# Tile loads in halves, released 48 records behind the begins of TensorE's 256-record blocks

## Chip, cores and metric

One core of a Trainium2 chip runs the whole kernel. The metric is the device time of one execution in microseconds. Before and after are compared by the medians of several runs.

## What is computed

Retention over q, k and v (8 batches, 8 heads, 576 positions, 64 per head, fp32), and then a mixture of experts with two levels of routing: 4 groups of 4 experts, one expert per token, 4608 tokens of 512 values, a hidden layer of 1024.

```python
# retention
scores = q @ k.transpose(0, 1, 3, 2) / sqrt(64)
gamma  = 1 - 2.0 ** (-5 - arange(8))
rel    = pos[:, None] - pos[None, :]
x      = (scores * where(rel >= 0, gamma ** rel, 0)) @ v
# mixture of experts, for each token of x (4608 x 512)
g = argmax(x @ w_group);  e = argmax(x @ w_expert[g])
y = softmax weight of g * softmax weight of e * (relu(x @ w1[g, e]) @ w2[g, e])
```

## The kernel before

**Two stages.** The first computes the retention of 36 tiles of 128 tokens (NT = 36, nine to a pair of batches; the ninth, marked m, holds the last 64 tokens of both) and routes their tokens. The second runs the experts' two layers, one pass per expert. The change lies in the first.

**One step per tile.** The loop at L968 goes over t from 0 to 36. Step t issues to TensorE, in this order: `av(t - 1)` (L911, the products of scores and values, eight matmuls into px), `state(t)` (L890, the product of keys and values, pst), `inter(t - 1)` (L926, what the state adds to px), `scores(t + 1)` (L842, into pss), the transposition of tile t - 6 (`xnat_pe`, L430, pxt), and every third step the logits and the routing of a group of three tiles. In the first steps the order differs a little. Tiles marked m have no state of their own. `scale(t + 1)` (L833) lets ScalarE multiply that tile's values before. VectorE masks the scores and turns px into x. GpSimd stores the rows of x into `xs`, sorted by expert, with indirect DMAs.

**Order.** All engines but TensorE are wrapped in `Ordered` (L113): what they are given keeps the order of the program, SP's loads too. TensorE is scheduled by hand, in program order (`pe = nc.tensor`, L129). Since every operation of a wrapped engine is recorded in the wrapper, rows of ScalarE, VectorE, GpSimd and SP have L124.

**Loads.** A tile is 1 MB in fp32: two planes of q and k, transposed, and two of v and k (`a`, tag "r", 7 buffers, RB). `loads(t)` (L727) issues it on SP, most tiles in one DMA of 1 MB; tiles 0, 1, 2 and the m tiles come in two DMAs. Before the loop six tiles are asked for (LOADS - 1, L809). In step t, behind `av(t - 1)`, `loads(t + 6)` (L989) follows. Its buffer was that of tile t - 1, so SP waits there until the last reader of that tile is done; where no `inter` reads it, a dependency on its `av` is added by hand.

**First weights.** The expert with the most tokens so far is chosen in step 28 (`pick`, PICK = 23, r = t - 23 = 5), and its number is read into a register of SP in step 29 (`expert_of(0)`, L1034). `xload(0)` in step 30 asks for its rows, and waits for their stores. `load_piece(0)` to `load_piece(3)` in steps 30 to 33 (L1042) ask for four weight pieces of 1 MB, in the same ring of buffers as the tiles, behind `xload(0)` on SP. `layer1(0, 0)` (L1047) uses the first piece in step 35.

**Matmuls as records.** The profile has one weight load and one matmul for a transposition or for a matmul of bf16 or fp32r operands, and two of each for a matmul of fp32: the eight of `av` stand as x16.

Of the kernel before, what the change touches and what calls it, by code (L numbers as in the profile page):

```python
# [7 lines left out]
F32 = mybir.dt.float32  # L8
# [7 lines left out]
P = 128  # L16
RG = 3
B, H, S, D = 8, 8, 576, 64
# [16 lines left out]
PICK = 23  # L35
WHOLE = 2
RB = 7
LOADS = 7
WARM = 7
TURNED = 2  # L40

FULL = 5
# [30 lines left out]
def moe_retention(ctx, tc, qkv, wgt, w, c_f, out):  # L73
# [52 lines left out]

            return call

    pe = nc.tensor  # L129
    dve, act, pool, sp = [Ordered(e_) for e_ in (nc.vector, nc.scalar, nc.gpsimd, nc.sync)]  # L130

    def apart(key, inst):
# [586 lines left out]
    with ExitStack() as ac:  # L719
# [4 lines left out]
        pss = ps_s.tile([P, 2, 4 * P], F32, name="pss")  # L724
        ps_x = ac.enter_context(tc.tile_pool(name="ps_x", bufs=1, space=PSUM))

        def loads(t):  # L727
            if t >= NT:
                return
            T = tiles[t]  # L730
            a = wp.tile([P, 4, DM], F32, name=f"a_{t}", tag="r", bufs=RB)
            n = 3 if T["m"] else 4
            if t < 2:
                flat = qkv[t].rearrange("h p c d -> (h p c d)")
                for i, j in (0, 2), (2, 3):
                    part = flat[i * P * DM : j * P * DM]
                    sp.dma_start(a[:, i:j], part.rearrange("(p c d) -> p c d", p=P, c=j - i))
            else:
                if t == 2:
                    for i in range(2):  # L740
                        i_ = sp.dma_start(a[:, 2 * i : 2 * i + 2], qkv[t, i])
                elif T["m"]:
                    sp.dma_start(a[:, 2:3], qkv[t, 1, :, 0:1])
                    i_ = sp.dma_start(a[:, 0:2], qkv[t, 0])
                else:
                    i_ = sp.dma_start(
                        a.rearrange("p (h c) d -> p h c d", h=2), qkv[t].rearrange("h p c d -> p h c d")
                    )
            u = t - RB
            if u > 0 and tiles[u]["S"] == [None]:  # L750

                tc.add_manual_dep(
                    i_.ins, tiles[u]["av"].name,
                    mybir.DependencyInfo(mybir.DependencyClass.Sync, mybir.DependencyReason.DATA),
                    reason="one tile a step",
                )
            T["qT"], T["kT"] = [a[:, i].rearrange("p (i j) -> p i j", i=NP) for i in range(2)]
            T["v"], T["k"] = [a[:, i].rearrange("p (h d) -> p h d", h=H) for i in (2, 3)]

        masks = dc.tile([P, 2, 2, P], F32, name="masks")  # L760
        rel = masks[:, 1].bitcast(I32)
# [44 lines left out]
        make_masks()  # L806
        act.dma_start(cf[:, 0:KC_ID], c_f[:, 0:KC_ID])
        act.activation(warm, warm, AF.Exp)
        for t in range(LOADS - 1):  # L809
            loads(t)  # L810

            if t == 3:
                sp.dma_start(wgp, wgt.rearrange("p (c e) -> p c e", c=NKC))
                sp.dma_start(cf[:, KC_EID:KC_TRI], c_f[:, KC_EID:KC_TRI])
# [27 lines left out]
        def scores(t):  # L842

            T = tiles[t]
            T["pss"] = pss
            if t == 0:
                T["pss"] = ps_x.tile([P, 2, 4 * P], F32, name="pss_0", tag="x")
            ps = T["pss"]  # L850
            whole = NP if t < FULL else 0
            for i in range(0, NP - whole, 2):
                for late in range(2):
                    for par in range(2):
                        for o in range(2):
                            k_ = slice((late ^ par) * D, (late ^ par) * D + D)
                            r = slice(o * D, o * D + D)
                            to = late * D + D if T["m"] else P
                            pe.matmul(  # L859
                                ps[k_, o, (i + par) * P + late * D : (i + par) * P + to],  # L860
                                T["kT"][r, i + par, k_], T["qT"][r, i + par, late * D : to],
                                start=True, stop=True,
                            )
            for i in range(NP - whole, NP):
                for o in range(2):
                    r = slice(o * D, o * D + D)
                    pe.matmul(  # L867
                        ps[:, o, i * P : i * P + P], T["kT"][r, i, :], T["qT"][r, i, :],
                        start=True, stop=True,
                    )  # L870
# [11 lines left out]
        def kturn(t):  # L882

            T = tiles[t]
            pk = ps_tr.tile([P, NP, P], F32, name=f"pk_{t}", tag="tr")
            for i in range(NP):
                pe.transpose(pk[:, i, :], T["kT"][:, i, :], ident)
            act.copy(T["k"].rearrange("p (i o) d -> p i (o d)", o=2), pk)

        def state(t):  # L890

            T = tiles[t]
            if T["m"]:
                T["S"] = [cur.pop(0)[1], cur.pop(1)[1]]
                return
            bi = T["j"] // 4
            first = bi not in cur
            T["S"] = [None if first else cur[bi][1]]
            pst = ps_st.tile([P, NP, D], F32, name=f"pst_{t}", tag="tr") if first else cur[bi][0]
            for i in range(NP):  # L900
                for o in range(2):
                    h = 2 * i + o
                    pe.matmul(  # L903
                        pst[o * D : o * D + D, i, :], T["k"][:, h, :], T["vs"][:, h, :],
                        start=first and i == 0, stop=True, skip_group_check=True,
                    )
            st = ap.tile([P, NP, D], F32, name=f"st_{t}", tag="st", bufs=5)
            act.copy(st, pst)
            cur[bi] = (pst, st)

        def av(t):  # L911

            T = tiles[t]
            px = ps_x.tile([P, 2, 4 * P], F32, name=f"px_{t}", tag="x")
            for s in range(2):
                for o in range(2):
                    for g in range(2):
                        T["av"] = pe.matmul(  # L918
                            px[g * D : g * D + D, o, s * P : s * P + P],
                            T["vs"][:, 4 * s + 2 * g + o, :], T["sT"][:, o, 2 * s + g, :],  # L920
                            start=s == 0, stop=True, skip_group_check=True,
                        )
            T["av"] = T["av"].ins
            T["px"] = px

        def inter(t):  # L926
# [38 lines left out]
        masked(0)  # L965
        first_gq((6,))
        kturn(0)
        for t in range(NT + 1):  # L968
            now = t < NT
            r = t - PICK  # L970

            if last_of_group(t - 4):
                choose(t - 4)
# [12 lines left out]
                scale(t + 1)  # L986
            if t:
                av(t - 1)
            loads(t + LOADS - 1)  # L989
            if 0 < t < TURNED:  # L990
                kturn(t)
            if now and not opening:
# [45 lines left out]
            if r == 11:  # L1038
                pick(1)
                expert_of(1)  # L1040
            if 6 < r < 11:
                load_piece(r - 7)  # L1042
            if t == NT - 1:
                load_piece(4, tiles[t - 6]["row"])
            if t == NT - 1:

                layer1(0, 0)  # L1047

    mc = ExitStack()
    psy = mc.enter_context(tc.tile_pool(name="psy", bufs=1, space=PSUM))  # L1050
    mp = mc.enter_context(tc.tile_pool(name="mp", bufs=2))
# [596 lines left out]
```

## Time and profile before

| | us |
|---|---|
| median of 3 runs | 563.97 |
| lowest, highest | 563.22, 566.93 |
| the profiled execution, its own time | 565.27 |
| its span, first to last instruction | 563.40 |
| TensorE matmuls busy in it | 548.6 (97%) |
| VectorE, ScalarE, GpSimd busy | 426.0, 330.4, 258.3 |

The span is what the profile's rows cover; the profiled execution's own time is 1.87 us more. The granted clock of TensorE was 0.998 of full speed over the span. TensorE's busy time counts matmuls from their start to a modelled end, so they overlap; an idle time of its row is time in which no matmul was under way. PE is TensorE's matmuls, PEld its weight loads.

### The profile page before, as it was taken

What the parts mean: (1) busy time and instruction counts of PE and PEld (TensorE: products, weight loads), DVE (VectorE), ACT (ScalarE), POOL (GpSimd) and SP (SyncE); (2) the same over time, 40 slices, a digit from 0 to 9 for tenths busy, and PEclk for the clock granted to TensorE, in tenths of its full rate; (3) what the DMA queues carried; (4) which work ended last, traced back from release to release, by engine and by line L of the source; (5) the groups of instructions that cost most, each with busy time, mean ns of one, the idle gap of its engine ahead of it and who ended that gap; (6) DMA issues with size and microseconds to landing.
All of it is one profiled execution on the core that took longest, in us unless ns stands there. A gap on an engine that the chain in (4) does not pass through costs nothing.

```text
span 563.4 us, 16624 instructions
## 1 busy us (share of the span) xinstructions
PE 548.6 (97%) x6149; PEld 520.8 (92%) x6149; DVE 426.0 (76%) x1000; ACT 330.4 (59%) x858; POOL 258.3 (46%) x394
## 2 busy tenths in 40 slices
PE   8998999899999999999999999999999999999995
PEld 6887888788689999999999999999999999999995
DVE  6886777788889678976767686877778687787783
ACT  7687877787565545454545454555555455555563
POOL 0023323253521138454554638373664836638565
PEclk9999999999999999999999999999999999999999
DMA  8998999969766893837465674839476584855831
GB/s 337 416 409 313 311 375 325 356 227 333 263 205 262 222 330 84 322 107 292 131 275 149 259 234 174 301 119 340 108 297 205 200 283 141 337 186 216 298 144 43
DMA packets 51001, 139.84 MB, mean 248 GB/s; under 512 B 7922, under 2 KB 28154, under 8 KB 42193
## 3 DMA queue, kind: packets, MB, share of 16 engines
q1 hardware_dynamic: 41648, 118.28, 58.9%
q0 software_dynamic: 9104, 20.07, 9.8%
q8 instruction: 73, 1.20, 0.8%
q14 instruction: 32, 0.25, 0.1%
q10 hardware_dynamic: 144, 0.05, 0.0%
HBM read 118.31 MB, written 24.55 MB: 254 GB/s over the span
## 4 chain that ended last, share of the span: by engine, by line
PE 95%; issue 2%; POOL 1%; DMA 1%; SPq 0%; POOLq 0%; ACT 0%; ACTq 0%
PE ph L695 35%; PE py L1147 11%; PE py L1146 11%; PE py L1148 11%; PE px L918 7%; PE pss L859 4%; PE pxt L437 4%; PE px L937 3%; PE pst L903 3%; PE py L1135 2%; PE plt L487 2%; PE phn L1203 1%; POOL out L124 1%; DMA a<-in_qkv 1%; PE pss L867 1%
## 5 line engine op out<-in xcount | busy, mean ns | idle before, releaser
L124 POOL DMA_INDIRECT out<-y,ii x148 | 161.1, 1089 | 58.8 <-issue 29.2
L124 DVE TENSOR_TENSOR wl<-r,wh 128x512 fp32r<-128x512 f32 x268 | 172.5, 685 | 6.0 <-ACT wh L124 3.1
L124 ACT ACTIVATE hh<-ph 128x320 fp32r<-128x320 f32 (+14 forms) x128 | 53.4, 417 | 182.1 <-PE ph L695 134.9
L124 ACT CAST wh<-r 128x512 fp32r<-128x512 f32 x268 | 151.7, 617 | 1.1 <-DMA r<-in_w 1.1
L695 PE MATMUL ph<-xTh_m,wh 128*128 128x316 f32 (+14 forms) x504 | 147.3, 292 | 0.0
L695 PE MATMUL ph<-xTl_m,wh 128*128 128x316 f32 (+13 forms) x504 | 147.3, 292 | 0.0
L695 PE MATMUL ph<-xTh_m,wl 128*128 128x316 f32 (+13 forms) x504 | 146.7, 291 | 0.0
L1147 PE MATMUL py<-hh,wl 128*128 128x316 f32 (+11 forms) x480 | 140.4, 293 | 0.0
L1146 PE MATMUL py<-hh,wh 128*128 128x316 f32 (+14 forms) x480 | 140.3, 292 | 0.0
L1148 PE MATMUL py<-hl,wh 128*128 128x316 f32 (+11 forms) x480 | 139.9, 291 | 0.0
L124 DVE SCALAR_TENSOR_TENSOR hl<-ph,hh 128x320 fp32r<-128x320 f32 (+13 forms) x126 | 58.0, 460 | 84.3 <-ACT hh L124 83.8
L695 PEld LDWEIGHTS ph<-xTh_m,wh 128*128 128x128 f32 x504 | 94.9, 188 | 0.7 <-issue 0.3
L695 PEld LDWEIGHTS ph<-xTl_m,wh 128*128 128x128 f32 x504 | 95.0, 188 | 0.2
L695 PEld LDWEIGHTS ph<-xTh_m,wl 128*128 128x128 f32 x504 | 95.0, 188 | 0.0
L1147 PEld LDWEIGHTS py<-hh,wl 128*128 128x128 f32 x480 | 90.4, 188 | 0.0
L1148 PEld LDWEIGHTS py<-hl,wh 128*128 128x128 f32 x480 | 90.3, 188 | 0.0
L1146 PEld LDWEIGHTS py<-hh,wh 128*128 128x128 f32 x480 | 90.3, 188 | 0.0
L124 POOL COPY pace<-hh 1x1 f32<-1x1 f32 x137 | 32.3, 236 | 119.7 <-ACT hh L124 119.0
L124 POOL DMA_INDIRECT xs<-xt,sl x33 | 32.6, 989 | 92.6 <-DVE xT L124 35.0
L124 ACT ACTIVATE vs<-a,cf 128x64 f32<-128x64 f32 x288 | 72.4, 336 | 2.7 <-DMA a<-in_qkv 2.7
L124 DVE TENSOR_TENSOR sT<-pss,masks 128x512 f32<-128x512 f32 x72 | 46.1, 682 | 9.4 <-PE pss L859 6.6
L918 PE MATMUL px<-sT,vs 128*64 128x128 f32 x576 | 39.5, 279 | 0.4 <-issue 0.3
(210 smaller groups left out, 611.3 us busy)
## 6 DMA issues: line engine op xcount, KB each, us to landing
r<-in_w SPq DMA_DIRECT2D x68, 1024.0 KB, 8.8
a<-in_qkv SPq DMA_DIRECT2D x29, 1024.0 KB, 9.5
xb<-xs SPq DMA_DIRECT2D x32, 165.0 KB, 3.9
a<-in_qkv SPq DMA_DIRECT2D x8, 512.0 KB, 6.5
xb<-xs SPq DMA_DIRECT2D x20, 148.5 KB, 3.3
out<-y,ii POOLq DMA_INDIRECT x148, 2.8
a<-in_qkv SPq DMA_DIRECT2D x6, 256.0 KB, 5.2
xb<-xs SPq DMA_DIRECT2D x8, 132.0 KB, 3.0
```

What stands on the lines that cost most here:

```text
L124: i_ = f(*a, **k)
L437: pe.transpose(T["pxt"][:, i, :], T["xT"][:, i, :], ident)
L487: pe.matmul(plt[32 * i : 32 * i + 32], wgp[:, i, :], tiles[t]["xTg"][:, i], start=True, stop=True)
L695: pe.matmul(ph[:, :v], a[:, kc, cs], b[:, kc, :v], start=n == 0, stop=n == 3 * NKC - 1)
L859: pe.matmul(ps[k_, o, (i + par) * P + late * D : (i + par) * P + to], T["kT"][r, i + par, k_], T["qT"][r, i + par, late * D : to], start=T ...
L903: pe.matmul(pst[o * D : o * D + D, i, :], T["k"][:, h, :], T["vs"][:, h, :], start=first and i == 0, stop=True, skip_group_check=True,)
L918: T["av"] = pe.matmul(px[g * D : g * D + D, o, s * P : s * P + P], T["vs"][:, 4 * s + 2 * g + o, :], T["sT"][:, o, 2 * s + g, :], start=s ...
L937: pe.matmul(px[g * D : g * D + D, o, s * P + r * w : s * P + r * w + w], st[rows, 2 * s + g, :], T["qT"][rows, 2 * s + g, r * w : r * w + ...
L1135: pe.matmul(py[:n], a[:, r0 : r0 + n], b[:, f % 2, :], start=st_ and m == 0, stop=sp_ and m == len(ab) - 1,)
L1146: pe.matmul(py[:, :w0], wh[:, f % 2, ds_], hh[:, :w0], start=st_, stop=False)
L1147: pe.matmul(py[:, :w], wl[:, f % 2, ds_], hh[:, :w], start=False, stop=False)
L1148: pe.matmul(py[:, :w], wh[:, f % 2, ds_], hl[:, :w], start=False, stop=sp_)
```

## The change

`Blocks` wraps TensorE and counts records: 2 for each call, 4 for a matmul whose stationary operand is plain fp32, 1 more by hand in `scores` and in `state`. Whenever the count passes 240 + 256 k, the instruction that passed it is given to `block`. `block` works out how far the loads may be asked: the step, plus the share of the step that is done (175 records to a step), plus a lead of 5.0 that grows to 5.8 over the first 25 steps, and not further than five tiles ahead of the step's own. Up to there it issues half tiles (`load(t, part)`, part 0 q and k, part 1 v and k), and weight pieces behind the tiles; each of these DMAs waits on SP until that instruction of TensorE is done. The call of `loads` in the step, the dependency on `av` and the pieces of steps 30 to 33 are gone. The six tiles ahead of the loop remain, as halves. What is still unasked of the four pieces is asked in step 35.

```diff
-LOADS = 7
 WARM = 7
+BLOCK, BLOCK0 = 256, 192 + 48
+FIRST = 6
+LEAD = (5.0, 0.8, 25)
...
-    pe = nc.tensor
+    class Blocks:
+
+        def __init__(self, engine, begin):
+            self.engine, self.n, self.turn = engine, begin, None
+
+        def records(self, n):
+
+            new = (self.n + n - BLOCK0) // BLOCK > (self.n - BLOCK0) // BLOCK
+            self.n += n
+            return new
+
+        def __getattr__(self, name):
+            f = getattr(self.engine, name)
+
+            def call(*a, **k):
+                i_ = f(*a, **k)
+                wide_ = name == "matmul" and a[1].dtype == F32
+                if self.records(4 if wide_ else 2) and self.turn:
+                    self.turn(i_)
+                return i_
+
+            return call
+
+    pe = Blocks(nc.tensor, 2)
...
-        def loads(t):
-            if t >= NT:
-                return
+        def load(t, part, behind=None):
+
             T = tiles[t]
-            a = wp.tile([P, 4, DM], F32, name=f"a_{t}", tag="r", bufs=RB)
...
+            if part == 0:
+                a = T["a"] = wp.tile([P, 4, DM], F32, name=f"a_{t}", tag="r", bufs=RB)
...
+            if t < TURNED:
                 flat = qkv[t].rearrange("h p c d -> (h p c d)")
...
+                i, j = ((0, 2), (2, 3))[part]
+                i_ = sp.dma_start(
+                    a[:, i:j], flat[i * P * DM : j * P * DM].rearrange("(p c d) -> p c d", p=P, c=j - i)
+                )
+            elif T["m"] and part:
+                i_ = sp.dma_start(a[:, 2:3], qkv[t, 1, :, 0:1])
             else:
...
-                    i_ = sp.dma_start(
-                        a.rearrange("p (h c) d -> p h c d", h=2), qkv[t].rearrange("h p c d -> p h c d")
-                    )
-            u = t - RB
-            if u > 0 and tiles[u]["S"] == [None]:
+                i_ = sp.dma_start(a[:, 2 * part : 2 * part + 2], qkv[t, part])
+            if behind is not None:
 
                 tc.add_manual_dep(
-                    i_.ins, tiles[u]["av"].name,
+                    i_.ins, behind.name,
                     mybir.DependencyInfo(mybir.DependencyClass.Sync, mybir.DependencyReason.DATA),
...
+        asked = {"half": 2 * FIRST, "piece": 0}
+
+        def block(i_):
+
+            t = now_at["t"]
+            far = t + (pe.n - now_at["n"]) / 175 + LEAD[0] + LEAD[1] * min(1, t / LEAD[2])
+            while asked["half"] < min(int(2 * far), 2 * (t + 6), 2 * NT):
+                load(*divmod(asked["half"], 2), i_.ins)
+                asked["half"] += 1
+            while asked["piece"] < min(int(far + 0.5) - NT, NPIECE):
+                load_piece(asked["piece"], i_.ins)
+                asked["piece"] += 1
+
+        now_at = {}
...
-        for t in range(LOADS - 1):
-            loads(t)
+        for t in range(FIRST):
+            for part in range(2):
+                load(t, part)
...
             T = tiles[t]
+            pe.records(1)
             T["pss"] = pss
...
             first = bi not in cur
+            if t >= TURNED:
+                pe.records(1)
...
         kturn(0)
+        pe.turn = block
         for t in range(NT + 1):
             now = t < NT
             r = t - PICK
+            now_at.update(t=t, n=pe.n)
...
                 av(t - 1)
-            loads(t + LOADS - 1)
...
-            if 6 < r < 11:
-                load_piece(r - 7)
             if t == NT - 1:
+                while asked["piece"] < NPIECE:
+                    load_piece(asked["piece"])
+                    asked["piece"] += 1
                 load_piece(4, tiles[t - 6]["row"])
...
+    pe.turn = None
```

## Rows read from the trace of the kernel before

**Rows 1.** Busy time by stretch (us, busy us of each engine with instructions, PEclk, DMA share, GB/s)

```profile
0.00:20.00 20.00, 18.21 (x291) 14.02 (x295) 13.38 (x32) 14.51 (x53) 1.13 (x9) 1.00 0.92 361
...
120.00:140.00 20.00, 19.70 (x465) 16.74 (x460) 17.35 (x56) 15.77 (x55) 8.39 (x16) 1.00 0.79 272
...
160.00:540.00 380.00, 380.00 (x2907) 378.22 (x2906) 289.31 (x608) 198.92 (x428) 198.61 (x289) 1.00 0.65 227
```

**Rows 2.** Waits of TensorE's matmuls, 10 to 140 us (total us, times, longest)

```profile
PE pss L859 <- issue: 5.0, 5, 2.0
PE pxt L437 <- issue: 0.9, 1, 0.9
PE px L918 <- issue: 0.3, 1, 0.3
PE pst L903 <- issue: 0.3, 1, 0.3
```

**Rows 3.** Busy time by stretch, cut at the ends of TensorE's gaps (engines as in rows 1: PE, PEld, DVE, ACT, POOL)

```profile
22.51:28.24 5.73, 4.85 (x134) 4.28 (x131) 5.03 (x16) 3.23 (x15) 0.00 (x0) 1.00 1.03 415
28.24:39.48 11.24, 10.54 (x255) 8.84 (x254) 9.04 (x28) 9.51 (x34) 3.47 (x5) 1.00 1.02 407
...
46.16:52.54 6.38, 5.09 (x127) 4.47 (x127) 5.03 (x16) 4.10 (x16) 1.60 (x5) 1.00 0.92 307
52.54:74.69 22.15, 21.58 (x509) 18.51 (x509) 16.61 (x44) 17.49 (x61) 6.79 (x11) 1.00 0.91 320
103.56:110.57 7.01, 5.00 (x132) 4.29 (x128) 5.03 (x16) 5.05 (x20) 2.15 (x3) 1.00 0.99 366
110.57:126.73 16.16, 16.14 (x379) 14.10 (x383) 13.03 (x40) 12.23 (x43) 7.72 (x18) 1.00 0.70 253
```

**Rows 4.** Chain that ended last, 0 to 140 us (start, us, what; each px begins a step)

```profile
24.35 1.02 PE px L918 x16
...
27.36 0.89 issue
...
32.78 1.02 PE px L918 x16
...
44.43 1.02 PE px L918 x16
...
51.26 1.29 issue
...
68.49 1.02 PE px L918 x16
...
74.13 0.57 issue
...
79.77 1.02 PE px L918 x16
...
108.56 2.03 issue
...
115.99 1.02 PE px L918 x16
...
138.27 1.09 PE px L918 x16
```

**Rows 5.** DMA queues, 25.9 to 27.0 us (packets, MB, share of 16 engines)

```profile
q8 instruction: 1, 0.02, 5.4%
```

**Rows 6.** DMA queues: first line 20 to 36 us, the others 36 to 120 us

```profile
DMA packets 1769, 6.55 MB, mean 410 GB/s; under 512 B 113, under 2 KB 113, under 8 KB 1765
...
q1 hardware_dynamic: 5841, 21.83, 74.3%
q0 software_dynamic: 1831, 6.19, 18.7%
```

**Rows 7.** SP's instructions in order of time, 112 to 150 us (start, us, merged)

```profile
125.77 2.69 SPq L124 DMA_DIRECT2D xb<-xs  x4
...
129.79 17.62 SPq L124 DMA_DIRECT2D r<-in_w  x5
```

## Prediction of the time after

> **What bounds the kernel now.** I looked first at the table of stretches. From 160 to 540 us TensorE is busy 380.00 of 380.00 us, at a granted clock of 1.00, so nothing can be won there except by an earlier start. From 0 to 140 us it is not: 18.21 us in the first 20 and 19.70 in the last [rows 1]. The change lies in that first stage, where each of the 36 steps does the retention of one tile.
>
> Next I asked what TensorE waits for between 10 and 140 us. Four lines answer: 5.0, 0.9, 0.3 and 0.3 us, 6.5 us in eight waits, all of them "issue", which means that no engine and no DMA released them [rows 2]. The reader should be struck by this: no wait for a tile, for VectorE or for ScalarE among the matmuls of the whole stage. The chain of waits shows the same pieces, 0.89 us at 27.36, 2.03 us at 108.56 [rows 4].
>
> Then I cut the time at the ends of these gaps and counted instructions [rows 3]. From the end of one to the next there are 255 + 254, 127 + 127, 509 + 509 matmuls and weight loads; with one or two semaphore records per tile, which the table doesn't count, these are 512, 256 and 1024. So the gaps fall every time on a multiple of 256 records, on different lines of the program, and not at every multiple: three blocks from 110.57 to 126.73 run through. That is how an engine looks whose program arrives in blocks of 256 and sometimes late. The DMA rows fit: a queue named "instruction" moves one 16 KB packet between 25.9 and 27.0 us, taking 5.4% of 16 engines for 1.1 us, 0.95 us on one engine, and the gap ends at 28.25 [rows 4, 5]. The block before began at 22.51, so this packet started at least 3.4 us into it. The DMA engines were full then, share 1.03 at 415 GB/s, and 0.99 in the block ahead of the longest gap; in the undisturbed three blocks the share was 0.70 [rows 3].
>
> The rule that I read from this: the next block's packet is asked about when a block begins, needs 0.95 us, and TensorE goes on some 1.35 us after it ends. A block takes 16.16 / 3 = 5.4 us [rows 3]. So the packet must start within 5.4 - 0.95 - 1.35 = 3.1 us of the begin. It starts later when tile loads stand before it.
>
> **What the gaps cost.** The eight gaps sum to 6.5 us [rows 2], a floor, since after each one the matmul pipe also refills. Steps of one position in the nine-step pattern can be compared: steps 29 to 35 take 138.27 - 115.99 = 22.28 us with one gap of 0.3 at the end, 21.98 without; steps 11 to 17 take 68.49 - 44.43 = 24.06, which is 2.08 more, though their gaps are 0.3 and 1.29 [rows 2, 4]. So each gap costs 0.25 us beyond itself: 6.5 + 8 x 0.25 = 8.5. A ceiling: steps 17 to 20 take 11.28 with one gap of 0.57 + 0.25, so 10.46 without, and nine steps 32.4; the 27 steps from 32.78 to 138.27 took 105.49 against 97.3 [rows 4], 8.2 lost, and with the gap at 27.36 (1.1) 9.3. I take 8.5, the value built from the gaps themselves; ends 6.5 and 9.3.
>
> **The change part by part.**
>
> *The loads of tiles 6 to 35 move.* Before, each is asked when a buffer comes free, anywhere in a block. After, an instruction 48 records into a block releases two to four halves: 48/256 x 5.4 = 1.0 us after the begin. I walked the 36 steps with the diff's counting (2 records for a transposition or a bf16 matmul, 4 for a plain matmul, 1 more per score and per state): 23 such instructions, five with four halves, the others with at most three. First packets follow an issue by about 1.5 us (the first 20 us have a share of 0.92, so 1.6 us are empty [rows 1]). Three halves are 1.57 MB, 3.8 us at 410 GB/s; the stores of rows, 6.19 MB in 84 us, are 0.40 MB a block, 1.0 us [rows 6]. So this work is over 1.0 + 1.5 + 3.8 + 1.0 = 7.3 us after the begin, 1.9 after the next one. The next packet can then start within its 3.1 us, even if it waits for everything. With four halves it is 3.2: late by 0.1. Since stores come in bunches, I leave 0.7 us for such begins. Bounds for what remains of the stalls: 0 and 4.3 (half).
>
> [...] In the saturated block from 22.51 the packet started 3.4 us late or more [rows 3, 5], about what 1.4 MB take at 410 GB/s [rows 6]. [...]
>
> *More DMAs.* Some 29 whole loads become 58. SP issues four row loads in 2.69 us [rows 7], 0.7 us each, less than the 1.3 us that a half then takes on the DMA engines, which hide it. Were it not hidden, three halves would land up to 1.4 us later, with steps to spare. Cost 0.
>
> *SP waits for TensorE.* Behind a waiting load on SP stand only later loads, the register load and row loads for the first expert, and the weight pieces. The row loads are issued at 125.77, the pieces from 129.79 [rows 7]. By my walk the first piece is released in step 30, ahead of those row loads, the second in step 32, two in step 33, near where they were in the program's own terms; layer 1 needs the first only at the end of step 35. Cost 0; between -0.5 (the first piece lands sooner) and +1.
>
> *Tiles are asked later.* Tile 6 is asked in step 2, tiles 7 and 8 in step 4, near 18.3 us. The first six tiles and constants are 6.0 MB, at 361 GB/s over 20 us [rows 1] there until about 17 us, tile 6 until 19.6, so the queue hardly runs empty. Tile 7 lands at about 22.5 and is scaled in step 6, from 24.35 on [rows 4]: 1.9 us to spare. Later tiles have 3 us and more. Cost 0; if the margin fails, 1 to 2 us a tile for two tiles.
>
> *More semaphore records.* A state now waits for its own half, one record more on TensorE in some 28 tiles. Cost 0, since a record without work needn't hold up the matmuls; up to a record's mean share of a block, 28 x 5.4/256 = 0.6 us.
>
> **Sum.** 8.5 - 0.7 = 7.8 us less. What is late next is nothing in the matmuls' rows: steps 29 to 35 show the undisturbed pace, and it held for six steps. Everything from 140 us on only starts earlier. The profiled execution took 565.27 us with a span of 563.40; 565.27 - 7.8 = 557.5. It lies 1.3 over the median of 563.97; part of such spread may itself be late code, so I move down by 0.5, not 1.3: **557.0**. Changes under 1%, 5.6 us, can hardly be told from none here.
>
> **The rivals.**
> 1. *Half comes back.* The tail of one block's halves and stores meets the next packet, or tile 7 arrives late. For: mean traffic from 36 to 120 us is already 334 GB/s, and 8 us less makes it 7% denser. Against: 410 GB/s were sustained [rows 6]. If 4.3 us of stalls stay: 561.
> 2. *Slower: the bursts starve the code.* If halves asked together move at 300 GB/s, not 410, three take 5.2 us and stores 1.3: over at 3.6 after the next begin, 0.5 late, 17 times; four take 7.0, 2.3 late, five times: 20 us of stalls, 11.5 more than now, 575. It decides from about 3.5 us after a begin on average. Against: traffic of mixed loads and stores reached 407 [rows 3].
> 3. *The count slips*, and loads go out ahead of a begin. My walk counts up to 27 records too many by step 35 if a state needs no record of its own; 48 leaves 21. So it would take more. Time as before, 564.
> 4. *The gaps aren't code*, but something in the program that stands every 256 records, so the order of the loads doesn't matter: 564. Against: different lines, and gaps from 0.3 to 2.03 us. [...]
>
> **How the numbers follow.** Forecast 0.66, rival 1 0.20, rival 2 0.05, rival 3 0.05, rival 4 0.04. The range takes in the forecast with its ends (9.3 us off the median is 554.7, a little lower for the spread) and rival 1: 553.5 to 562.5. Faster by over 1% means under 558.3: nearly all of the forecast and a third of rival 1, 0.69. Slower 0.05, the rest, 0.26, within 1%.
>
> **What would show it.** Right: the matmuls' "issue" waits between 10 and 140 us fall from 6.5 us to under 1; steps 11 to 17 take near 22.0; the score-value products of step 35 start about 8 us sooner than 138.27; from there to the end it takes as long as before. Wrong: gaps still on multiples of 256 with a share near 1.0 there (rivals 1, 2); TensorE or ScalarE waiting for a tile, above all 6 or 7; gaps moved to other lines but as long (rival 3, 4).

## The result: slower by 1%, and the profile after

| | us |
|---|---|
| before, median of 12 runs | 564.61 (562.73 to 566.93) |
| after, median of 12 runs | 570.01 (567.62 to 573.45) |
| ratio, 95% interval | 1.0101 [1.0077, 1.0125] |
| the profiled execution of after, its own time | 573.17 |
| its span | 571.4 |

The forecast was 557.0 with a range of 553.5 to 562.5, so it was wrong in its sign. The two profiled executions differ by 7.9 us, the medians by 5.4; the profiled one of after is a long one of its kernel.

In three of the six sets of runs behind this document every kernel, the one before included, took some 10 us more; ratios are therefore taken within a set, and each comes with the time of the kernel before in that set. A ratio is the measurement's own estimate with its 95% interval and can differ from the quotient of the medians (by 0.3% in set 3).

First, what TensorE's matmuls wait for between 10 and 150 us (line, total us, times, longest). In after:

```profile
PE pss L146 <- issue: 8.2, 4, 3.3
PE px L146 <- issue: 3.4, 3, 1.5
PE plt L146 <- issue: 0.9, 1, 0.9
```

All of it is "issue" as in [rows 2], but 12.5 us instead of 6.5, in eight waits as before, which are longer. (Operations of TensorE now have L146, those of the other engines L126, since both are recorded in a wrapper.)

The chain that ended last shows where these waits lie (start, us, what; an "x16" or "x32" of px here begins a step, as in [rows 4]). In after:

```profile
26.50 0.67 PE pss L146 x31
27.17 3.33 issue
...
37.98 1.67 PE px L146 x32
...
48.49 1.02 PE px L146 x16
...
77.14 1.76 issue
...
84.18 1.02 PE px L146 x16
...
119.87 1.42 issue
...
131.24 2.12 issue
...
144.31 0.94 issue
...
147.00 1.62 PE px L146 x32
```

Counted in records, the eight longest pauses end at 961, 2754, 3009, 3777, 4289, 4802, 5313 and 5825, all 193 or 194 more than a multiple of 256. They are begins of blocks, as before, three of them the very ones that were late there (961, 3009 and 5825); the code is still late, only more so. Against [rows 4], step 11 begins 4.1 us later (48.49 against 44.43), step 20 4.4 us, step 35 8.7 us (147.00 against 138.27). From step 35 to the end it takes 424.4 us (571.4 - 147.0) against 425.1 (563.4 - 138.27), so the whole loss lies in the first stage.

Two stretches make most of it. The six steps from 29 to 35 hold the pauses of 1.42, 2.12 and 0.94; with 0.25 us more for each, what a gap cost beyond itself in the steps of the kernel before [rows 4], that is 5.2 us, and these steps, begun at 119.62, indeed took 5.1 more than before. The other stretch is the first pause. The table of stretches in after around it (columns as in [rows 1]):

```profile
18.70:23.50 4.80, 4.80 (x132) 3.97 (x132) 4.74 (x12) 4.11 (x17) 0.00 (x0) 1.00 0.81 283
23.50:28.20 4.70, 3.67 (x106) 3.23 (x99) 4.00 (x14) 2.20 (x11) 0.00 (x0) 1.00 1.02 361
28.20:30.50 2.30, 0.01 (x1) 0.00 (x0) 1.00 (x6) 1.05 (x5) 0.00 (x0) 0.81 0.70 277
30.50:33.30 2.80, 2.80 (x24) 2.49 (x25) 1.80 (x5) 1.46 (x5) 0.00 (x0) 0.50 0.09 31
...
29.70:36.40 6.70, 5.91 (x90) 5.47 (x89) 2.33 (x6) 2.96 (x10) 1.12 (x1) 0.50 0.29 68
36.50:39.10 2.60, 2.60 (x42) 1.60 (x37) 1.35 (x3) 1.74 (x5) 0.38 (x1) 1.00 1.02 416
```

Read it downwards. From 23.50 to 28.20 the DMA engines are full (share 1.02). TensorE stands from 27.17 to 30.50. Then two more things go wrong that the prediction had not priced. The granted clock falls within the pause of 3.33 us to 0.50, where it is from 29.70 to 36.40, and it is at 1.00 from 36.50. From the end of the pause to the begin of step 8 it therefore takes 7.5 us (37.98 - 30.50), in the kernel before 4.5 (32.78 - 28.25 [rows 4]). And the DMA engines run dry (share 0.09 from 30.50 to 33.30), because the next release hangs on a TensorE that stood still. What still moves there is this (queue: packets, MB, share of 16 engines):

```profile
q1 hardware_dynamic: 20, 0.07, 6.1%
```

A share of 6.1% is about what one engine of the sixteen, busy all the time, would show, and it holds for most of the stretch: 0.06 from 30.50 to 31.50 and again from 32.00 to 32.50 (25 GB/s). So the last of these loads come up to some 3 us behind the bulk. The trace doesn't name the engines, so whether one of them was behind the others, and whether the late packets were on such a one, is not shown. The later pauses, up to 2.12 us, leave the clock at 1.00 in this run.

Now the code packet itself. The DMA rows of after, first from 18.7 to 23.5, then from 28.2 to 29.3 us (issues: line, count, KB each, us to landing; queues: packets, MB, share of 16 engines):

```profile
a<-in_qkv SPq DMA_DIRECT2D x3, 512.0 KB, 7.5
a<-in_qkv SPq DMA_DIRECT2D x1, 256.0 KB, 9.2
...
q1 hardware_dynamic: 116, 0.43, 97.0%
q8 instruction: 1, 0.02, 5.4%
```

The block that stalls began at 22.54. Its successor's packet started at 28.23, 5.7 us later. Three and a half halves (1.84 MB) were released from 18.73 on, another three (1.57 MB) from 23.68 on, both where the change puts them, 47 records behind a begin. Of these 3.41 MB at most 0.72 were still moved behind 28.2 (2.30 x 277 + 2.80 x 31 kB; the next release is only at 33.9). So 2.7 MB went ahead of the packet, at least 0.8 MB of them of the release that came after its block's begin. With the DMA engines nearly empty, a share of 0.09 from 30.50 to 33.30, the next one came sooner: its block began at 30.50, and it started at 31.54, 1.04 us later.

Over the stage, the packets that start 3.5 us or more behind a begin rise from 6 to 9 (of the 21 blocks begun at records 449 to 5569). The DMA traffic that makes them late is no denser than before: from 36 to 120 us queue 1 in after has

```profile
q1 hardware_dynamic: 6245, 22.23, 75.4%
```

against 74.3% in [rows 6]. Only its order changed.

### The profile page after: what moved, and what is told of

It reads as the page before. It is cut to its first block, busy times and chain, and to the rows that moved or that the text cites. A ratio compares the mean times of both kernels' runs of the same rounds, so it can differ in the third digit from the quotient of the medians.

```text
span 571.4 us, 16685 instructions
## 1 busy us (share of the span) xinstructions
PE 551.2 (96%) x6149; PEld 523.3 (92%) x6149; DVE 426.0 (75%) x1000; ACT 330.7 (58%) x858; POOL 257.6 (45%) x394
## 4 chain that ended last, share of the span: by engine, by line
PE 92%; issue 3%; DVE 3%; POOL 1%; DMA 1%; POOLq 0%; DVEq 0%
PE ph L146 35%; PE py L146 35%; PE px L146 9%; PE pss L146 4%; PE pxt L146 3%; PE pst L146 2%; PE plt L146 2%; DVE sT L126 1%; PE phn L146 1%; POOL out L126 1%; DMA a<-in_qkv 1%; PE pl L146 1%; DVE xT L126 1%; PE pp L146 0%; PE pk L146 0%
## 5 line engine op out<-in xcount | busy, mean ns | idle before, releaser
L126 POOL DMA_INDIRECT out<-y,ii x148 | 161.0, 1088 | 59.1 <-issue 29.4
L126 DVE TENSOR_TENSOR wl<-r,wh 128x512 fp32r<-128x512 f32 x268 | 172.4, 685 | 5.2 <-ACT wh L126 2.3
L126 ACT ACTIVATE hh<-ph 128x320 fp32r<-128x320 f32 (+14 forms) x128 | 53.5, 418 | 184.3 <-PE ph L146 137.6
L126 ACT CAST wh<-r 128x512 fp32r<-128x512 f32 x268 | 151.6, 617 | 0.0
L146 PE MATMUL ph<-xTl_m,wh 128*128 128x316 f32 (+13 forms) x504 | 147.3, 292 | 0.0
L146 PE MATMUL ph<-xTh_m,wh 128*128 128x316 f32 (+14 forms) x504 | 147.3, 292 | 0.0
L146 PE MATMUL ph<-xTh_m,wl 128*128 128x316 f32 (+13 forms) x504 | 146.7, 291 | 0.0
L146 PE MATMUL py<-hh,wl 128*128 128x316 f32 (+11 forms) x480 | 140.4, 293 | 0.0
L146 PE MATMUL py<-hh,wh 128*128 128x316 f32 (+14 forms) x480 | 140.3, 292 | 0.0
L146 PE MATMUL py<-hl,wh 128*128 128x316 f32 (+11 forms) x480 | 139.9, 291 | 0.0
L126 DVE SCALAR_TENSOR_TENSOR hl<-ph,hh 128x320 fp32r<-128x320 f32 (+13 forms) x126 | 58.0, 460 | 85.7 <-ACT hh L126 85.2
L146 PEld LDWEIGHTS ph<-xTh_m,wh 128*128 128x128 f32 x504 | 94.9, 188 | 0.7 <-issue 0.3
L146 PEld LDWEIGHTS ph<-xTl_m,wh 128*128 128x128 f32 x504 | 95.0, 188 | 0.2
L146 PEld LDWEIGHTS ph<-xTh_m,wl 128*128 128x128 f32 x504 | 95.0, 188 | 0.0
L146 PEld LDWEIGHTS py<-hh,wl 128*128 128x128 f32 x480 | 90.4, 188 | 0.0
L146 PEld LDWEIGHTS py<-hl,wh 128*128 128x128 f32 x480 | 90.3, 188 | 0.0
L146 PEld LDWEIGHTS py<-hh,wh 128*128 128x128 f32 x480 | 90.3, 188 | 0.0
L126 POOL COPY pace<-hh 1x1 f32<-1x1 f32 x137 | 32.3, 236 | 120.4 <-ACT hh L126 119.7
L126 POOL DMA_INDIRECT xs<-xt,sl x33 | 32.6, 989 | 111.2 <-DVE ob L126 44.7
L126 ACT ACTIVATE vs<-a,cf 128x64 f32<-128x64 f32 x288 | 72.4, 335 | 2.9 <-DMA a<-in_qkv 2.9
L126 DVE TENSOR_TENSOR sT<-pss,masks 128x512 f32<-128x512 f32 x72 | 46.1, 682 | 11.4 <-PE pss L146 11.0
L146 PE MATMUL px<-sT,vs 128*64 128x128 f32 x576 | 41.0, 283 | 3.6 <-issue 3.4
```

The lines of the kernel that those rows point to most:

```text
L126: i_ = f(*a, **k)
L146: i_ = f(*a, **k)
```

## Experiments

Theory: a code packet is late when much of a release is still on its way as the packet is asked for. Then the size of a release and its moment in the block decide. Rivals: that the halves themselves cost something, that code isn't the cause, or that only one of size and moment matters.

**Set 1 (before: 575.42 us, 25 runs).** Even spread, so that halves go out one at a time:

```diff
-BLOCK, BLOCK0 = 256, 192 + 48
+BLOCK, BLOCK0 = 44, 0
```

> The changed kernel with the release looked at every 44 records instead of every 256, so halves go out one at a time, evenly, with no regard to the begins of blocks. Burst theory (a code packet waits for all that stands before it on its DMA engine; three or four halves released together are not through when the next packet is asked, and then the next burst comes in front of it too): the queue is seldom deeper than one half, 1.3 us, so stalls at begins fall under 2 us of the 11.5 us in the profile after, time 556 to 560. Halves theory (more and smaller DMAs are what hurts, whenever they are asked): 568 to 572 as after. Density theory (only the sum of the traffic counts): 564 to 570.

577.55 us, 1.003 [1.0002, 1.0058]; issue waits 6.1 us between 10 and 150 us, 3.9 of them at begins, where the burst theory had under 2. They are about those of the kernel before (6.5 and 5.3 us in two of its profiles). Nothing is won without bursts. Whether the change's loss is gone isn't shown: this set has no run of the change, which in the two other sets of the longer kind has 1.0017 and 1.0042.

The kernel before with nothing but its loads cut in halves:

```diff
-                if t == 2:
+                if not T["m"]:
```

> The kernel before with its whole-tile loads issued as two halves, at the moments of before (when a buffer comes free). Burst theory: two halves behind each other are one tile, the same as before, 562 to 566. Halves theory: most of the loss appears, 568 to 572. Density theory: 564.

575.26 us, 0.998 [0.9948, 1.0013]: the cut alone, with its DMAs and records, costs nothing that can be measured. It also wins nothing: issue waits of 4.2 us were left, and the time is the same.

The moment of release moved to 144, and to 224, records behind a begin:

```diff
-BLOCK, BLOCK0 = 256, 192 + 48
+BLOCK, BLOCK0 = 256, 192 + 144
```

> The changed kernel with the release 144 records behind a begin, not 48: 3.0 us after the begin, so the halves reach the DMA engines some 1.5 us later, 4.5 us after it, just ahead of the moment (4 to 5.4 us) at which the next packet is asked. Burst theory: nearly every packet waits for a whole burst, 4 to 5 us, stalls of 1 to 2 us at 22 begins, 580 to 595. Halves and density theory: no difference from after, 568 to 572.

> The changed kernel with the release 224 records behind a begin, 32 ahead of the next: the halves reach the DMA engines about 0.8 us after that next begin, just behind the packet that is asked there, and have until the following request, over 4 us, to get through. Burst theory: the earlier burst is nearly through when the packet is asked, few stalls, 557 to 563. Halves and density theory: no difference from after, 568 to 572.

144: 583.26 us (4 runs), 1.0134 [1.0089, 1.0179], issue waits 11.4 us. 224: 576.28 us, 1.0028 [0.9986, 1.007], issue waits 4.1 us and one wait of 1.0 us behind a tile that came late. Both lose one release (the count passed the mark in a record added by hand, where nothing hangs on it), so each has one release of six halves; they differ in size as well as in moment and prove neither.

**Set 2 (before: 576.5 us, 13 runs).** Before and after once more, and two kernels in which loads are left out: tiles 7 to 35 (f3), or the odd ones among them but for 9 and 27 (f4). Their steps use the data of earlier tiles, and the loop over the rest of an overfull expert is left out, so the second stage has other sizes and only the first can be compared.

```diff
-            a = wp.tile([P, 4, DM], F32, name=f"a_{t}", tag="r", bufs=RB)
+            if t >= 7:
+                a = tiles[2 + t % 5 if t < 30 else 5 + t % 2]["a"]
...
+                return
+            a = T["a"] = wp.tile([P, 4, DM], F32, name=f"a_{t}", tag="r", bufs=RB)
```

> The kernel before once more, as the control for the other runs on this chip. Both theories: gaps of TensorE's matmuls with no releaser between 10 and 145 us of 4 to 9 us, all at multiples of 256 records, and the ratio 1.00.

> The changed kernel once more beside its control. Burst theory: gaps at begins of 10 to 15 us, 4 to 8 us more than the control, and the time more by the same 4 to 8 us, ratio 1.007 to 1.014. If the loss were elsewhere (more records, SP, the weights), the gaps would be as in the control and the time still longer.

> The kernel before without the loads of tiles 7 to 35: those steps work on tiles 2 to 6 again, and the loop for tokens over the caps is left out, so only the first stage can be read. Theory that code waits behind loads: no gaps at begins from step 8 on, steps 11 to 17 in 22.0 us, step 35 reached some 8 us sooner than in the control. Rival (the gaps are the code stream's own, whatever the loads do): gaps at multiples of 256 records as in the control, step 35 where the control has it.

> The kernel before with the loads of every odd tile from 7 on left out (the step works on the tile before it again, but behind the tiles marked m), and the loop for tokens over the caps left out: half the traffic of loads, whole tiles as before. Queue theory: a packet of code waits for a tile of 2.6 us at most, so gaps under 1.5 us in sum. If only the peak of the queue counts and not its mean, as many gaps as tiles in flight at a begin, 3 to 5 us.

After: 577.57 us, 1.0017 [0.9981, 1.0052]. TensorE's waits between 10 and 150 us in the kernel without loads:

```profile
PE pss L864 <- issue: 1.5, 5, 0.4
PE px L942 <- issue: 0.4, 1, 0.4
PE px L923 <- DVE xT L124: 0.3, 1, 0.3
```

None of these pauses stands at a begin of a block, and all 21 packets start within 2.4 us of their begin, some up to 0.7 us ahead of it. So the pauses at multiples of 256 are code that waits behind loads, and the prediction's rival 4 falls. With a DMA share of 0.19 from 36 to 120 us no begin shows a pause; in the kernel before, with 0.94 in the same stretch, begins do (6.5 us of waits from 10 to 140 us [rows 2]). With half the loads out, issue waits are 3.6 us, against 5.3 in the kernel before. But step 35 begins at 139.19 us without loads, at 139.50 in that set's kernel before: only 0.3 us sooner, though that kernel's begins had 2.5 us of pauses (0.9, 0.9 and 0.7). In that set little was to be won from the code. Where the other 2 us went stays open.

**Set 3 (before: 566.09 us, 25 runs).** Before and after, and after with at most three halves a release:

```diff
+            most = asked["half"] + 3
-            while asked["half"] < min(int(2 * far), 2 * (t + 6), 2 * NT):
+            while asked["half"] < min(int(2 * far), 2 * (t + 6), 2 * NT, most):
```

> The kernel before again, as the control on the chip of this call. All theories: gaps at begins of 3 to 9 us in sum from 10 to 145 us, the largest under 2.3 us.

> The changed kernel as the control on the chip of this call. Burst theory: ratio 1.002 to 1.013; a first gap of 2.5 to 3.5 us in front of record 961, a granted clock under 1.00 in the stretch from 20 to 40 us after it, and the other large gaps one block behind a release of four halves.

> The changed kernel with at most three halves to a release (the fourth goes with the next). Burst theory: the gaps one block behind the four-half releases (6.1 us of the profile after) shrink to under 2 us, the first gap of 3.3 us shrinks too, since it stands behind 3.5 and then three halves; time 3 to 7 us under the changed kernel of the same call, gaps at begins 3 to 6 us. If it is not the size of the bursts: the same as the changed kernel, within 2 us.

After: 571.43 us, 1.0066 [1.0021, 1.011]. Capped: 564.44 us, 1.0004 [0.9965, 1.0043]. In this set the cap takes the whole loss back. Waits on issue between 10 and 150 us, first in after, then in the capped kernel:

```profile
PE pss L146 <- issue: 6.9, 4, 2.2
PE px L146 <- issue: 2.1, 2, 1.5
PE plt L146 <- issue: 0.9, 1, 0.9
PE pst L146 <- issue: 0.3, 1, 0.3
```

```profile
PE pss L146 <- issue: 4.4, 5, 1.4
PE px L146 <- issue: 1.0, 1, 1.0
```

Issue waits fall from 10.2 to 5.4 us, late packets from 7 to 4, and step 35 begins at 137.15 instead of 144.35. (The kernel before has 9 late packets in its profile of this set, 3.6 to 4.9 us behind their begins, and issue waits of 4.8 us.) The first long pause is gone, and with it the fall of the clock (0.91 from 20 to 40 us in after in that set, 1.00 in the capped kernel).

228 records behind a begin, with no release lost:

> The changed kernel released 228 records behind a begin, 28 ahead of the next. Burst theory: as with 224, no gap over 1.3 us, gaps at begins under 4 us, 3 to 8 us under the changed kernel of the same call and ratio to before 0.992 to 1.002. If the moment in the block doesn't matter: the same as the changed kernel.

572.87 us, 1.0104 [1.006, 1.0148], with issue waits of 14.6 us, the longest of all, and 14 late packets. The theory had expected under 4 us here, as at 224, which four records sooner had 4.1 us and 3 late packets. Here releases are of four and two halves by turns, so that size and moment are mixed again; why 224 and 228 differ so much stays open.

**Set 4 (before: 575.58 us, 23 runs).** The cap at 48; the same cap at 128; at most two halves every 128 records; after itself.

```diff
-BLOCK, BLOCK0 = 256, 192 + 48
+BLOCK, BLOCK0 = 256, 192 + 128
```

> At most three halves to a release, 48 records behind a begin. Size theory (four halves at once keep the code waiting past two begins): 3 to 8 us under the changed kernel of this call, ratio to before 0.995 to 1.005. If the first run with the cap was chance: within 2 us of the changed kernel.

> The cap of three with the release 128 records behind a begin, so only the moment changes against the run before. Size theory: within 3 us of it, since engines busy nine tenths of the time have a tail in front of the packet at any moment. Moment theory (a release just ahead of the request for the next packet is what hurts): stalls of 0.5 to 1.5 us at most begins, 8 to 20 us more.

> At most two halves to a release, one release every 128 records, 48 and 176 behind a begin. Size theory: shorter queues, gaps at begins under those of the cap of three, 0 to 4 us less time than it. If total traffic sets the stalls once no release is of four: the same as the cap of three within 2 us.

> The changed kernel as control on the chip of this call: ratio 1.000 to 1.013, gaps at begins of 8 to 15 us in its profile.

Cap at 48: 577.62 us, 1.0049 [1.0015, 1.0083]. Cap at 128: 586.81 us (4 runs), 1.0221 [1.0174, 1.0268]. Two every 128: 581.95 us (4 runs), 1.0112 [1.0073, 1.0152]. After: 578.18 us, 1.0042 [1.0015, 1.0069]. Waits on issue between 10 and 150 us with the cap at 128:

```profile
PE pss L146 <- issue: 5.6, 7, 1.8
PE px L146 <- issue: 4.5, 4, 2.0
PE plt L146 <- issue: 0.6, 1, 0.6
PE pxt L146 <- issue: 0.4, 1, 0.4
```

and with the same cap at 48:

```profile
PE pss L146 <- issue: 2.5, 7, 0.6
PE plt L146 <- issue: 1.1, 1, 1.1
PE px L146 <- issue: 0.4, 1, 0.4
```

11.1 us against 4.0, and 11 late packets against 5, where SP issues three halves at nearly every release in both: at equal size, the moment matters. Smaller releases don't help when half of them go out 80 records ahead of the next begin (8.1 us of waits and 12 late packets with two halves every 128 records). But the cap's gain of set 3 didn't return. Its issue waits are again below those of after (4.0 against 6.7), and its time is the same.

**Set 5 (before: 565.46 us, 23 runs).** The cap once more, and the cap at 8 records behind a begin:

```diff
-BLOCK, BLOCK0 = 256, 192 + 48
+BLOCK, BLOCK0 = 256, 192 + 8
```

> At most three halves a release, but released 8 records behind a begin instead of 48, which is 40 records or 0.85 us sooner. Theory of the moment (what counts is how much of a release is still on the DMA engines when the next block's packet is asked for): the tail past the next begin shortens by 0.85 us, so the packets of late blocks start up to 0.85 us sooner after their begin than with 48, the issue waits between 10 and 150 us fall from the 4 to 6 us of the other run of this call to 1 to 3 us, and the time is 2 to 4 us under it: a ratio to the kernel before of 0.995 to 1.000. Rival (the packet waits for whatever new burst reaches the queue near it, so an earlier release meets the same block's packet too): no gain or worse, issue waits of 4 us and more, ratio 1.002 to 1.010.

> At most three halves a release, 48 behind a begin, once more on another chip. If the cap takes the change's loss back, as on the chip where after took 571.4 and the capped kernel 564.4, the ratio to the kernel before is 0.998 to 1.002 here too. If that was the state of that chip, and the cap decides nothing, the ratio is that of the change itself on four chips, 1.002 to 1.010, as on the last one (1.005).

Cap at 48: 564.08 us, 0.9975 [0.9948, 1.0002]. Cap at 8: 564.54 us, 0.9977 [0.9939, 1.0015]. So in both sets of the shorter kind in which it ran (3 and 5), the capped kernel is no slower than the kernel before, while the change was slower by 1.0% and 0.7% in the two in which it ran (the first and 3). In the one set of the longer kind in which both ran, they were alike. Neither capped version beats the kernel before by more than the measurement can tell.

The profiled execution of the cap at 48 in this set is the longest of its 13 runs, 571.82 us. It has issue waits of 7.2 us, 9 late packets, and three falls of the granted clock to 0.50, behind pauses of 1.68, 2.24 and 2.05 us. So the cap doesn't remove the long pauses from every execution.

At 8 the first stage behaves as the prediction wanted it. Waits of TensorE on issue between 10 and 150 us:

```profile
PE pss L146 <- issue: 1.4, 2, 1.1
PE px L146 <- issue: 0.7, 1, 0.7
```

2.1 us of issue waits, two late packets, and step 35 begins at 133.98 us, 4.3 sooner than in [rows 4]. Yet the span of this execution is 563.8 us, 0.4 longer than the kernel before had. The twelve runs of the cap at 8 fall into two groups: five took 560.0 to 560.9 us, seven 563.9 to 568.3, and the profiled one, 565.53, is of the seven. Of the 23 runs of the kernel before in this set one is under 562 us. So in some executions most of the 4.3 us may have reached the end; no trace shows one of them. In the profiled one, the stretch from 160 to 180 us, beside that of the kernel before, says where the 4.3 us went (columns as in [rows 1]):

```profile
160.00:180.00 20.00, 16.91 (x102) 14.85 (x101) 16.15 (x35) 10.65 (x22) 2.44 (x2) 1.00 0.60 216
```

```profile
160.00:180.00 20.00, 20.00 (x126) 18.41 (x125) 18.53 (x43) 13.24 (x27) 2.10 (x2) 1.00 0.61 217
```

TensorE does 102 matmuls there instead of 126. The chain of the run at 8 gives the reason:

```profile
129.00 4.07 DMA a<-in_qkv
...
157.81 5.38 DMA xs<-xt_last,sl
...
164.91 2.10 DMA xb<-xs
...
168.18 1.19 PE py L146 x4
```

The next expert's rows (xb) are loaded only when the last tile's rows of x are stored, and that last store starts at 157.81, as late as in the kernel before (157.3), although step 35 began 4.3 us sooner. TensorE waits 3.1 us for what hangs on it. The last tile itself did move along: ScalarE finishes its rows at 152.9 us, 3.6 sooner than in the kernel before (156.4). What did not are the DMAs. SP's instructions in the run at 8 (compare [rows 7]):

```profile
125.91 1.93 SPq L126 DMA_DIRECT2D xb<-xs  x4
...
129.00 0.38 SPq L126 DMA_DIRECT2D a<-in_qkv  x1
129.64 18.23 SPq L126 DMA_DIRECT2D r<-in_w  x5
```

The row loads of the first expert wait for a store of rows. The run at 8 issued it at 118.47 us, the kernel before at 122.31, but it landed at 125.79 and 125.66: the lead was gone. Behind the row loads stand on SP the last half tile, though the instruction of TensorE that releases it, by the count 8 records behind the begin at 121.68, ran at 122.05, and the weight pieces, as late as before (129.79). The DMA engines were full just before, those of the kernel before were not. From 120 to 125 us, first the run at 8, then the kernel before (columns as in [rows 1]):

```profile
120.00:125.00 5.00, 5.00 (x121) 4.00 (x120) 3.90 (x10) 4.90 (x18) 1.97 (x3) 1.00 0.99 361
```

```profile
120.00:125.00 5.00, 5.00 (x135) 4.75 (x133) 4.62 (x19) 3.89 (x15) 2.83 (x6) 1.00 0.66 224
```

The same happens once more with GpSimd's stores among the weight pieces, first in the run at 8, then in the kernel before:

```profile
138.39 0.99 POOL L126 DMA_INDIRECT xs<-xt,sl  x1 [0.43 <-DMA r<-in_w]
...
147.49 0.17 POOL L126 IOTA xt<- 128x16 int32 x1 [3.45 <-DMA xs<-xt,sl]
```

```profile
142.19 0.99 POOL L124 DMA_INDIRECT xs<-xt,sl  x1 [2.08 <-DMA r<-in_w]
...
146.93 0.16 POOL L124 IOTA xt<- 128x16 int32 x1 [0.51 <-DMA xs<-xt,sl]
```

Issued 3.8 us sooner, this store landed after 9.0 us instead of 4.7, and the stores behind it, those of the last tile among them, could go on only from 147.49 instead of 146.93. So in this execution the lead ended at the DMA engines. That they were the reason is read from the trace and not tested by a run of its own.

All profiled first stages, by the packets' starts (late: 3.5 us or more behind a begin), the issue waits between 10 and 150 us, and the begin of step 35; the ratio is that of all the kernel's runs. First the sets in which the kernel before took some 565 us:

| kernel | late of 21 | issue waits, us | step 35, us | ratio |
|---|---|---|---|---|
| cap 3 at 8 (set 5) | 2 | 2.1 | 134.0 | 0.9977 |
| before (set 3) | 9 | 4.8 | 139.2 | 1 |
| cap 3 at 48 (set 3) | 4 | 5.4 | 137.2 | 1.0004 |
| before (first) | 6 | 6.5 | 138.3 | 1 |
| cap 3 at 48 (set 5, longest run) | 9 | 7.2 | 143.0 | 0.9975 |
| after (set 3) | 7 | 10.2 | 144.4 | 1.0066 |
| after (first) | 9 | 12.5 | 147.0 | 1.0101 |
| after at 228 (set 3) | 14 | 14.6 | 150.5 | 1.0104 |

Then those in which it took some 575 us:

| kernel | late of 21 | issue waits, us | step 35, us | ratio |
|---|---|---|---|---|
| no loads (set 2) | 0 | 1.9 | 139.2 | |
| half the loads (set 2) | 3 | 3.6 | 140.7 | |
| cap 3 at 48 (set 4) | 5 | 4.0 | 143.1 | 1.0049 |
| after at 224 (set 1) | 3 | 4.1 | 142.5 | 1.0028 |
| before in halves (set 1) | 5 | 4.2 | 140.6 | 0.998 |
| before (set 2) | 4 | 5.3 | 139.5 | 1 |
| even spread (set 1) | 5 | 6.1 | 144.8 | 1.003 |
| after (set 2) | 6 | 6.2 | 144.2 | 1.0017 |
| after (set 4) | 6 | 6.7 | 143.6 | 1.0042 |
| two every 128 (set 4) | 12 | 8.1 | 145.9 | 1.0112 |
| cap 3 at 128 (set 4) | 11 | 11.1 | 149.3 | 1.0221 |
| after at 144 (set 1) | 14 | 11.4 | 149.6 | 1.0134 |

In both groups longer waits go by and large with a later step 35 and, from some 8 us on, with a longer time. The count of late packets follows them loosely. In the second group some 2 to 3 us of the waits stand at no begin (all 1.9 without loads, 2.9 of the 5.3 in the kernel before), so the two groups are not to be compared by them.

## Why the prediction was wrong, point by point

**What bounds the kernel.** Right. The pauses at multiples of 256 records are code, late behind loads: without loads no begin has one (f3). Rival 4 is out, and so is rival 3, since the releases fired 47 records behind their begins. What the prediction lacked is the next bound: with the pauses nearly gone, in the run at 8, the DMA engines have a share of 0.98 from 36 to 120 us, against 0.94 in the kernel before.

**The loads move: the step that failed.** The working said that three halves "are 1.57 MB, 3.8 us at 410 GB/s", that with the stores "this work is over 1.0 + 1.5 + 3.8 + 1.0 = 7.3 us after the begin", and that the packet "can then start within its 3.1 us, even if it waits for everything"; 0.7 us was left for the stalls. There were issue waits of 12.5 us. Two things in that sum were wrong. The rate was the best that [rows 6] has; while the two releases of the first pause were moved it was 283 GB/s (at a share of 0.81) and then 361 (at 1.02). That alone doesn't make the packets late: at the stage's mean, 334 GB/s, the same sum ends 3.0 us behind the next begin (1.0 + 1.5 + 4.7 + 1.2 - 5.4), still within 3.1. The other is that the work ahead of the packet was counted as one release with its tail. The release of the packet's own block comes 1.0 us behind the begin, and in the first pause at least 0.8 MB of it (3.41 - 0.72 - 1.84) went ahead of the packet too. The trace doesn't show when a packet is asked for, so "even if it waits for everything" was a guess about the order in a queue, and no row bounded it.

**Rival 2** (bursts starve the code; 575 us, a chance of 0.05) is what happened in mechanism and sign, at about half its price: 6.0 us of waits more, where it had 11.5. Its condition, packets later than some 3.5 us, holds for 9 of 21 begins. The prediction thought it unlikely because mixed traffic had reached 407 GB/s in one stretch, while the mean of the same stage, 334, stood in the text of rival 1.

**The first pause** was nowhere in the sum. At 3.33 us it cost twice: the pause, and some 3 us more (7.5 - 4.5) to the begin of step 8, with the clock at 0.50 until 36.4 us.

**More DMAs, more records, cost 0.** Right for the cut: the kernel before with halves has a ratio of 0.998 [0.9948, 1.0013].

**Tiles are asked later, cost 0.** Right between 10 and 150 us in after, whose waits name no tile. Asking late has another price, which the first pause shows: the DMA engines stand dry behind it (share 0.09 from 30.50 to 33.30), since a stalled TensorE releases nothing. What that cost in time isn't shown.

**"Everything from 140 us on only starts earlier"** was wrong too, though the change itself couldn't show it. The profiled run at 8 won 4.3 us in the first stage and lost them by 180 us, since the stores and the loads that wait for them came no sooner on full DMA engines (share 0.99 from 120 to 125 us). So even a correct first stage need not have given the 7.8 us of the sum. That the same traffic in less time is denser stood in rival 1, which priced it only as late code and a late tile.

**The size of what could be won.** The 8.5 us came from one execution. The kernel before had 6.5 us of issue waits in it, 4.8 (2.6, 1.3 and 0.9) in set 3, and 5.3 in set 2, of which 2.5 stood at begins. A single profile had stood for the kernel.

**Open:** why the cap gave 0.6% back in set 3 and nothing in set 4; why releases at 224 and 228 differ so much; what sets apart the five short executions of the cap at 8.

## What to carry to other kernels

Loads that are gathered into bursts to keep a window free must be through before that window opens at the stage's mean rate, not the best one (334 and 410 GB/s here), with the burst of the window itself counted; at equal size, moving the burst from 48 to 128 records behind a begin cost 1.7% here (1.0221 against 1.0049). If releases hang on an engine, a stall of that engine also starves the loads (a DMA share of 0.09 behind the pause of 3.33 us), so cap the size of a release and let it go early: that left the fewest waits of all versions with their loads here (2.1 us with the cap at 8), though no less time. And before a gain in one stage is booked to the end of the program, find the chain that the next stage hangs on, DMAs included: in the profiled execution with the best first stage, stores that landed late on full DMA engines (one after 9.0 us instead of 4.7) took back all that it had won.

## What the runs showed of the hardware that was not expected

- TensorE's granted clock fell to 0.50 behind some pauses and not behind others. In after it fell within the pause of 3.33 us and was at 1.00 again at 36.50 us, 6.0 us after TensorE had started again. In set 3 it was at 0.50 from 29.9 to 33.2 us, behind a pause of 2.23 us, and with the cap in set 5 behind pauses of 1.68, 2.24 and 2.05 us. Pauses of 2.12 us (at 131 us in after) and of 2.03 us (at 108 us in the kernel before) left it at 1.00. So the length of a pause alone didn't tell in these runs.
- At the end of a burst the last packets of loads came at about a sixteenth of the engines' rate for some 3 us: from 30.50 to 33.30 us in after, 20 of them took 6.1% of the 16 DMA engines.
- The same kernel took 565 us in some sets and 575 in others, on one chip number both times (sets 4 and 5). In the longer ones TensorE does fewer matmuls in the same time at the same granted clock. From 160 to 540 us the kernel before in set 2 has the following row, against 2907 matmuls in [rows 1]:

```profile
160.00:540.00 380.00, 377.64 (x2856) 373.48 (x2855) 286.09 (x602) 195.64 (x423) 193.18 (x282) 1.00 0.64 224
```

In its first stage there are also pauses of 0.2 to 0.5 us some 12 us apart (at 38.8, 50.8, 62.7, 73.6 and 86.6, then at 109.6, 122.9 and 134.5), at no particular record. What makes them is not known.
